# Whole-tensor loads, a pause in the load queue, and squares moved to the GpSimd engine, in a talking-heads attention and FFN kernel

## Chip, cores, metric

The kernel runs on one core of a Trainium2 chip; the sessions ran on different chips. The metric is device microseconds of that core for one execution. Executions of this kernel scatter more than those of many others: in six sessions the kernel before took between 602.3 and 613.0 us, without a run in the slower, disturbed state (runs in the undisturbed one are called "fast"). Ratios are computed as the mean time of one kernel's fast runs over the mean of the other's fast runs of the same rounds, with a 95% interval, so a ratio is not quite the ratio of the medians that are quoted beside it.

Engine names: PE is the matmul engine and PEld its weight loads, DVE the vector engine, ACT the scalar engine, POOL the GpSimd engine, SP the sync engine, which here only issues transfers.

## The reference

```python
# q, k, v: (8, 12, 448, 64) f32; w_pre, w_post: (12, 12)
def attention(q, k, v, w_pre, w_post):
    scores = (q @ k.transpose(0, 1, 3, 2)) / sqrt(64)
    scores = einsum('bhij,hg->bgij', scores, w_pre)        # mix the heads before the softmax
    attn = softmax(scores, axis=-1)
    attn = einsum('bhij,hg->bgij', attn, w_post)           # and again after it
    return attn @ v
# x: the attention output as (3584, 768); w_in: (768, 2048); w_out: (2048, 768)
def ffn(x, w_in, w_out):
    h = maximum(x @ w_in, 0.0)
    return (h * h) @ w_out
```

Inputs and output are f32; inside, the kernel works in bf16 with f32 accumulation.

## The kernel before

The 448 queries of a batch are 45 tiles of 10 queries; the program advances two tiles at a time. I call this a **double step** (ds), numbered from 0; a batch is 22.5 of them. For each tile:

- `score_pair` computes scores for a block of 128 queries and copies them to SBUF as `S` (half the copies on ACT, half on DVE).
- `gather` moves, for 10 queries, the scores of all 12 heads from `S` to 120 partitions of a buffer `G`: an SBUF-to-SBUF DMA of 105 KB in packets of 896 bytes. There are 12 `G` buffers, so gathers are issued 10 tiles ahead.
- `mix` multiplies `G` by the head-mixing weights (tile `m_ps`), ACT takes the exponential (`e_sb`) with its row sum, DVE the reciprocal (`rc`), POOL normalises (`d`). Two double steps later, `unmix` applies the second mixing (`at_ps`, copied by DVE to `at`).
- Attention times v (`ot_ps`, copied by ACT to `xt`), then the FFN: `h_ps`, relu (`hr`), square (`h`), `o_ps`. For the first batch the FFN's first half is done in pieces of 160, 160 and 128 queries as soon as these are ready.

q, k, v and the weights come from DRAM as f32 and become bf16 on the way: such casting transfers are issued by POOL, and they share one queue, called q0 below. Gathers are issued by SP (queue q1) or ACT (queue q10). q and k of a batch land in one staging buffer each (`qst`, `kst`), and PE transposes them (the **turn**, tile `tr_ps`). The turn of the second batch is due at double step 15, that of the third at 29 or 30.

PE and POOL take their work in the order of the program here (the traces below show it: a mix at 71.3 us stands behind transposes that wait until 69.8 us, and v is issued at 23.4 us, behind the first normalisation). So where in the program a load is issued decides when POOL gets to it.

```python
    def load(t, src, b, h0=0, h1=H):                 # heads h0..h1 of q, k or v
        nc.gpsimd.dma_start(out=t[0:PR, h0:h1, :, :].rearrange("p h r d -> p h (r d)"),
                            in_=src[b, h0:h1, :, :].rearrange("h (p r) d -> p h (r d)", r=R))
    ...
    def load_v(b, x):                                # thirds; load_qk the same, k and q in turn
        if x == 0:
            vs[b] = stage_tile("v", 2)
        load(vs[b], v, b, 4 * x, 4 * x + 4)
    def load_w1(x): ...                              # eighths of w_in, 384 KB each as bf16
    def load_w2(x): ...                              # eighths of w_out
    ...
        # in ffn1_unit, n = 160, 160, 128 queries for the first batch, S = 448 later
        square = nc.vector if n < S and ft % 4 else nc.gpsimd
        square.tensor_tensor(out=h2ts[(b, ft)][:, c0:c1], in0=hr[:, 0:n], in1=hr[:, 0:n], op=ALU.mult)
    ...
    def gather(k):
        ...
        eng = nc.scalar if b == 0 and k % 2 else nc.sync
        eng.dma_start(out=g[OFF:OFF + H * n, :], in_=Sb[(b, blk)][x:x + n, :, :])
    ...
        # at_load(i, f): f is issued before tile i; -1 is ahead of the first double step
        for x in range(2):
            at_load(-1, load_w1, x)
        for x in range(3):
            at_load(-1, load_v, 0, x)
            at_load(44 + x, load_v, 1, x)
        for x in range(2, 8):
            at_load(-1, load_w1, x)
        for x in range(8):
            at_load(18 + 2 * x + (6 if x > 3 else 0), load_w2, x)
        for x in range(6):
            at_load(6 + 2 * x, load_qk, 1, x)        # second batch
            at_load(46 + 2 * x, load_qk, 2, x)       # third batch
        ...                                          # later batches alike
        gathers_for(-1)                              # the first gathers
        for n in range(NPAIR, 2 * NPAIR):
            score_pair(n)                            # six more score pairs
        spin(8)                                      # matmuls whose result is not used
        for f in loads.get(-1, []):
            f()
        for ds in range(nd + LAG):
            for i in (2 * ds, 2 * ds + 1):
                for f in loads.get(i, []):
                    f()
            ...                                      # turn, unmix, attention times v as due
            scores_for(ds, ...)
            if now2:
                mix(ds)
            gathers_for(ds)
            ...
            fill(share)                              # FFN work
```

The softmax here doesn't subtract the row's maximum and nothing guards it: scores larger than these inputs give would overflow.

Of the kernel before, what the change touches and what calls it, by code (L numbers as in the profile page):

```python
# [14 lines left out]
B, H, S, D = 8, 12, 448, 64  # L15
DMODEL = H * D
DFF = 2048
NPAIR = H // 2
# [4 lines left out]
NT = 45  # L23
# [19 lines left out]
def kernel(  # L43
# [11 lines left out]
    nc = tc.nc  # L55
    P = nc.NUM_PARTITIONS
# [12 lines left out]
    def stage_tile(name, bufs):  # L69
        return stage.tile([P, H, R, D], BF16, name=name, tag=name, bufs=bufs)  # L70

    def load(t, src, b, h0=0, h1=H):
        nc.gpsimd.dma_start(out=t[0:PR, h0:h1, :, :].rearrange("p h r d -> p h (r d)"),
                            in_=src[b, h0:h1, :, :].rearrange("h (p r) d -> p h (r d)", r=R))

    staged, vs = {}, {}
# [58 lines left out]
    w1 = [wts.tile([P, NPAIR, DFF // 4], BF16, name=f"w1_{x}") for x in range(4)]  # L135
# [3 lines left out]
    def shared_half():  # L139
        return wts.tile([P, half2], BF16, name="w2_1", tag="w2_1", bufs=1)  # L140

    def w2_part(x):
        return w2[x][:, :].rearrange("p (c m) -> p c m", m=DMODEL)
# [63 lines left out]
    def av_units(b, part):  # L207
        return [(800, lambda cp=cp: av_unit(b, part, cp)) for cp in range(2)]

    def load_v(b, x):  # L210
        if x == 0:
            vs[b] = stage_tile("v", 2)
        load(vs[b], v, b, 4 * x, 4 * x + 4)

    def load_qk(b, x):
        if x == 0:
            kst = stage_tile("kst", 1)
            staged[b] = (stage_tile("qst", 1), kst)
        u, w = x // 2, 1 - x % 2
        load(staged[b][w], k if w else q, b, 4 * u, 4 * u + 4)  # L220

    def load_w1(x):
        n = DFF // 4
        h = NPAIR // 2
        c = x % 2 * h
        nc.gpsimd.dma_start(out=w1[x // 2][:, c:c + h, :],
                            in_=moe_w_in[128 * c:128 * c + 128 * h, n * (x // 2):n * (x // 2) + n].rearrange(
                                "(c p) f -> p c f", p=P))

    def load_w2(x):  # L230
        n = DFF // 8
        c = x % 4 * 2
        if x == 4:
            w2[1] = shared_half()
        nc.gpsimd.dma_start(out=w2_part(x // 4)[:, c:c + 2, :],
                            in_=moe_w_out[n * x:n * x + n, :].rearrange("(c p) m -> p c m", p=P))

    def ffn1_unit(b, ft, half, c0=0, c1=S):
        if half == 0:
            h_open[0] = bank("h_ps")  # L240
        ps = h_open[0]
        n = c1 - c0
        for c2 in range(3 * half, 3 * half + 3):
            nc.tensor.matmul(ps[:, 0:n], lhsT=w1[ft // 4][:, c2, ft % 4 * 128:ft % 4 * 128 + 128],  # L244
                             rhs=xts[b][:, c2, c0:c1], start=(c2 == 0), stop=(c2 == NPAIR - 1))
        if half == 0:
            return
        if (b, ft) not in h2ts:
            h2ts[(b, ft)] = ffnp.tile([P, S], BF16, name="h2", tag="h2", bufs=FT + 1)
        hr = ffnp.tile([P, S], F32, name="hr", tag="hr", bufs=2)  # L250
        if n < S and ft % 2:
            nc.vector.tensor_scalar_max(out=hr[:, 0:n], in0=ps[:, 0:n], scalar1=0.0)
        else:
            nc.scalar.activation(out=hr[:, 0:n], in_=ps[:, 0:n], func=ACT.Relu)  # L254
        square = nc.vector if n < S and ft % 4 else nc.gpsimd
        square.tensor_tensor(out=h2ts[(b, ft)][:, c0:c1], in0=hr[:, 0:n], in1=hr[:, 0:n], op=ALU.mult)  # L256

    h_open, o_open, osbs = {}, {}, {}
# [75 lines left out]
    def gather(k):  # L334

        b, t = steps[k]
        blk, tl = divmod(t, TPB)
        n = min(IQ, S - IQ * t)
        x = BLK_OFF[blk] + IQ * tl
        g = gts[k % len(gts)]  # L340
        eng = nc.scalar if b == 0 and k % 2 else nc.sync
        eng.dma_start(out=g[OFF:OFF + H * n, :], in_=Sb[(b, blk)][x:x + n, :, :])
        Gs[k] = g

# [61 lines left out]
    def spin(n):  # L406
        pss = [bank("spin_ps") for _ in range(2)]
        for _ in range(n):
            for z in (0, 64):
                rhs = ident[z:z + 64, 0:64].unsqueeze(1).to_broadcast([64, S // 64, 64])  # L410
                for x in (0, 64):
                    nc.tensor.matmul(pss[z // 64][x:x + 64, 0:S], lhsT=ident[z:z + 64, 0:64], rhs=rhs,
                                     start=True, stop=True)

    steps = [(b, t) for b in range(B) for t in range(NT)]
    with tc.manual_schedule(engines={PE, POOL}):
# [10 lines left out]
        def at_load(i, f, *args):  # L427
            loads.setdefault(i, []).append(lambda: f(*args))

        for x in range(2):  # L430
            at_load(-1, load_w1, x)
        for x in range(3):
            at_load(-1, load_v, 0, x)
            at_load(44 + x, load_v, 1, x)
        for x in range(2, 8):
            at_load(-1, load_w1, x)
        for x in range(8):
            at_load(18 + 2 * x + (6 if x > 3 else 0), load_w2, x)
        for x in range(6):
            at_load(6 + 2 * x, load_qk, 1, x)  # L440
            at_load(46 + 2 * x, load_qk, 2, x)
        for b in range(1, B):
            if b + 2 < B:
                for x in range(6):
                    at_load(NT * b + 22 + 2 * x, load_qk, b + 2, x)
            if b + 1 < B:
                for x in range(3):
                    at_load(NT * b + 34 + 2 * x, load_v, b + 1, x)
        nd = len(steps) // 2
        issued, gathered = [2 * NPAIR], [0]  # L450
        blocks = [(b, blk) for b in range(B) for blk in range(4)]
        starts = [NT * b + TPB * blk for b, blk in blocks] + [len(steps)]

        def scores_for(ds, most):
            tile = 2 * ds + AHEAD + 2
            blk = sum(tile >= x for x in starts) - 1
            if blk + 1 >= len(blocks):
                want = NPAIR * len(blocks)
            elif ds < 2 * NPAIR:
                want = 2 * NPAIR + 1 + ds  # L460
            elif blk in (3, 4):
                want = NPAIR * 4 + 2 * max(0, ds - FIRST_TURN[0])
            else:
                into, size = tile - starts[blk] - 2, starts[blk + 1] - starts[blk] - 2
                want = NPAIR * (blk + 1) + -(-NPAIR * into // size)
            want = min(want, issued[0] + most, NPAIR * min(blk + 2, len(blocks)))
            k = min(2 * ds + 8, len(steps) - 1)
            want = max(want, needs(steps[k]))
            while issued[0] < want and issued[0] % NPAIR < turned.get(issued[0] // (4 * NPAIR), 0):
                score_pair(issued[0])  # L470
                issued[0] += 1
# [6 lines left out]
                gathered[0] += 1  # L478

        gathers_for(-1)  # L480
        for n in range(NPAIR, 2 * NPAIR):
            score_pair(n)
        spin(8)
        for f in loads.get(-1, []):
            f()
        for ds in range(nd + LAG):
# [21 lines left out]
            if old2:  # L508
                unmix(ds - LAG)
                for b1, t1 in old2:  # L510
                    ends = PARTS[b1 % 2]
                    if t1 + 1 in ends:
# [3 lines left out]
                        if b1 == 0:  # L516
                            c = (IQ * ends[part], min(IQ * ends[part + 1], S))
# [47 lines left out]
```

## Time and profile before

| | us |
|---|---|
| median of the first 3 runs | 607.46 (605.88 to 608.25) |
| run in which the profile below was taken | 602.29 (span of the core 600.3) |
| a second profile of the same kernel, taken later | 609.92 (span 607.9) |

The head of the page of the kernel before: the span, then each engine's busy time, its share of the span and its instructions.

```profile
span 600.3 us, 27220 instructions
PE 557.1 (93%) x11346; PEld 316.7 (53%) x11346; DVE 432.8 (72%) x1123; ACT 395.5 (66%) x1196; POOL 397.0 (66%) x579
```

The chain of waits (the work that ended last, followed back from the end: start, duration, what) of the kernel before starts with the first loads and a few score copies, and then shows this:

```profile
17.82 6.77 DMA G<-S
24.61 0.80 ACTq L342
27.05 0.43 PE m_ps L351 x4
```

The chain stands for 6.77 us on one gather, while w_in and v move beside it; ACT issues one more gather (0.80 us); the first mix follows. The view of waits from 17 to 60 us says what ACT did meanwhile: it waited for that transfer in one piece.

```profile
engine line waited for: us in total, times, longest us
ACT S L325 <- DMA G<-S: 7.4, 1, 7.4
```

### The profile page before, as it was taken

To read this page: it belongs to the slowest core of one execution; us is meant where nothing else is said; L and a number is where in the kernel's file an instruction comes from. 1 tells how busy PE (TensorE), PEld (TensorE's weight loads), DVE (VectorE), ACT (ScalarE), POOL (GpSimd) and SP (SyncE) were. 2 spreads that over 40 slices of the span, in tenths; PEclk is the share of its full clock that TensorE was granted. 3 is DMA by queue.
4 is the path that set the end of the run, shared out by engine and by line. 5 is a ranking of instruction groups with operands and counts; after the bars stand their busy time and mean duration, and the time that the engine had idled before them with its cause. 6 is when DMAs were issued, how large, how long until landed. Compare 5 with 4: busy or idle time off the path is not lost.

```text
span 600.3 us, 27220 instructions
## 1 busy us (share of the span) xinstructions
PE 557.1 (93%) x11346; PEld 316.7 (53%) x11346; DVE 432.8 (72%) x1123; ACT 395.5 (66%) x1196; POOL 397.0 (66%) x579
## 2 busy tenths in 40 slices
PE   4698878988999999999999899999999999999996
PEld 3266555644655555545645455545655555555554
DVE  5488999987987688777786688777887787755101
ACT  2487677577778667876578656886678767962420
POOL 7288568466579945995479934996478846882440
PEclk9899999999999999999999999999999999999999
DMA  9999779589456965687446865588543655322002
GB/s 133 224 202 213 158 148 185 90 120 211 105 119 101 151 143 125 113 135 153 119 94 107 134 156 115 89 146 148 123 98 68 118 143 119 80 63 71 24 24 68
DMA packets 90912, 74.12 MB, mean 123 GB/s; under 512 B 6309, under 2 KB 87717, under 8 KB 90789
## 3 DMA queue, kind: packets, MB, share of 16 engines
q1 hardware_dynamic: 48982, 47.20, 33.2%
q0 software_dynamic: 38816, 22.81, 29.2%
q10 hardware_dynamic: 2990, 2.37, 1.2%
q8 instruction: 88, 1.44, 1.0%
q14 instruction: 36, 0.29, 0.1%
HBM read 45.63 MB, written 11.01 MB: 94 GB/s over the span
## 4 chain that ended last, share of the span: by engine, by line
PE 65%; POOL 10%; DVE 9%; DMA 7%; ACT 5%; issue 2%; ACTq 0%; DVEq 0%; POOLq 0%
PE o_ps L277 22%; PE h_ps L244 18%; PE at_ps L382 7%; PE ot_ps L193 6%; DMA G<-S 6%; PE m_ps L351 5%; POOL d L360 5%; DVE at L387 4%; PE s_ps L322 3%; POOL h L256 3%; PE tr_ps L170 3%; ACT e_sb L356 2%; ACT xt L204 2%; DVE S L325 2%; DMA qst<-in_q_dram 1%
## 5 line engine op out<-in xcount | busy, mean ns | idle before, releaser
L360 POOL TENSOR_SCALAR d<-e_sb,rc 128x448 bf16<-128x448 f32 x360 | 227.6, 644 | 158.5 <-DVE rc L358 156.6
L387 DVE CAST at<-at_ps 112x480 bf16<-112x480 f32 x360 | 219.2, 649 | 44.3 <-PE at_ps L382 42.0
L356 ACT ACTIVATE e_sb<-m_ps 128x448 f32<-128x448 f32 x360 | 195.8, 558 | 20.4 <-POOL d L360 9.9
L244 PE MATMUL h_ps<-xt,w 128*128 128x448 bf16 (+2 forms) x960 | 163.0, 316 | 3.6 <-DVE at L387 2.2
L277 PE MATMUL o_ps<-w,h 128*128 128x384 bf16 (+1 forms) x1024 | 161.6, 327 | 0.9 <-ACT xt L204 0.5
L325 ACT CAST S<-s_ps 128x448 bf16<-128x448 f32 x186 | 97.2, 540 | 74.0 <-PE s_ps L322 59.0
L244 PEld LDWEIGHTS <-w 128*128 128x128 bf16 x960 | 79.2, 98 | 80.2 <-issue 31.2
L277 PEld LDWEIGHTS <-h 128*128 128x128 bf16 (+1 forms) x1024 | 82.8, 101 | 72.0 <-issue 26.4
L256 POOL TENSOR_TENSOR h<-hr 128x448 bf16<-128x448 f32 (+2 forms) x124 | 109.1, 887 | 17.1 <-ACT hr L254 17.1
L325 DVE CAST S<-s_ps 128x448 bf16<-128x448 f32 x186 | 111.5, 613 | 3.3 <-PE s_ps L322 1.8
L382 PE MATMUL at_ps<-post,d 60*64 60x60 bf16 x5760 | 84.8, 194 | 7.3 <-POOL d L360 5.8
L382 PEld LDWEIGHTS <-d 60*64 60x64 bf16 x5760 | 63.6, 108 | 48.1 <-issue 18.7
L351 PE MATMUL m_ps<-G,pre 64*64 64x448 bf16 x720 | 77.5, 355 | 11.2 <-DVE at L387 2.6
L254 ACT ACTIVATE hr<-h_ps 128x448 f32<-128x448 f32 (+2 forms) x136 | 68.7, 511 | 27.5 <-PE h_ps L244 12.1
L356 ACT ACTIVATION_READ_ACCUMULATOR e_sb<-m_ps 128x1 f32 x360 | 78.1, 217 | 0.0
L204 ACT ACTIVATE xt<-ot_ps,bvec 128x160 bf16<-128x160 f32 (+3 forms) x144 | 44.6, 384 | 47.6 <-PE ot_ps L193 37.7
L322 PE MATMUL s_ps<-kT,qT 64*64 64x448 bf16 x768 | 70.4, 360 | 5.0 <-ACT S L325 3.9
L358 DVE RECIPROCAL rc<-sm 128x1 f32<-128x1 f32 x360 | 50.1, 154 | 33.1 <-ACT e_sb L356 31.2
L284 DVE COPY osb<-o_ps 128x384 f32<-128x384 f32 x48 | 26.0, 546 | 40.5 <-PE o_ps L277 40.4
L193 PE MATMUL ot_ps<-at,v 112*64 112x160 bf16 (+4 forms) x1152 | 46.1, 229 | 1.6 <-DVE at L387 1.4
L193 PEld LDWEIGHTS <-v 112*64 112x64 bf16 x1152 | 38.5, 109 | 14.6 <-issue 14.1
L351 PEld LDWEIGHTS <-pre 64*64 64x64 bf16 x720 | 28.2, 106 | 29.1 <-issue 27.2
(43 smaller groups left out, 239.2 us busy)
## 6 DMA issues: line engine op xcount, KB each, us to landing
G<-S SPq DMA_DIRECT2D x324, 105.0 KB
kst<-in_k_dram POOLq DMA_DIRECT2D x24, 224.0 KB, 6.1
qst<-in_q_dram POOLq DMA_DIRECT2D x24, 224.0 KB, 5.9
v<-in_v_dram POOLq DMA_DIRECT2D x24, 224.0 KB, 5.8
w<-in_moe_w_in_dram POOLq DMA_DIRECT2D x8, 384.0 KB, 16.6
w<-in_moe_w_out_dram POOLq DMA_DIRECT2D x8, 384.0 KB, 15.1
out_dram<-osb SPq DMA_DIRECT2D x8, 336.0 KB
out_dram<-osb SPq DMA_DIRECT2D x8, 288.0 KB
```

Source lines behind the costliest of these rows:

```text
L193: nc.tensor.matmul(ps[64 * hh:64 * hh + 64, TW * y + c0:TW * y + 2 + n], lhsT=vs[b][0:PR, g, r, :], rhs=at[0:PR, r, g, c0:2 + n], start=(y ...
L244: nc.tensor.matmul(ps[:, 0:n], lhsT=w1[ft // 4][:, c2, ft % 4 * 128:ft % 4 * 128 + 128], rhs=xts[b][:, c2, c0:c1], start=(c2 == 0), stop=( ...
L254: nc.scalar.activation(out=hr[:, 0:n], in_=ps[:, 0:n], func=ACT.Relu)
L256: square.tensor_tensor(out=h2ts[(b, ft)][:, c0:c1], in0=hr[:, 0:n], in1=hr[:, 0:n], op=ALU.mult)
L277: nc.tensor.matmul(dst, lhsT=h2ts[(b, ft)][:, mt * 128:mt * 128 + ROWS[mt]], rhs=w2_part(ft // 8)[:, ft % 8, n2 * 384:(n2 + 1) * 384], sta ...
L322: nc.tensor.matmul(pss[hh][z:z + 64, 0:S], lhsT=qTs[b][rs, p, q0:q0 + 64], rhs=kTs[b][rs, p, :], start=True, stop=True)
L325: copy(out=Sb[(b, blk)][:, 2 * p + hh, :], in_=pss[hh][:, 0:S])
L351: nc.tensor.matmul(pss[y][64 * x:64 * x + 64, 0:S], lhsT=pre[rows, :], rhs=gs[x][rows, :], start=True, stop=True)
L356: nc.scalar.activation(out=e[:, :], in_=pss[y][:, 0:S], func=ACT.Exp, scale=SCALE, accum_out=sm[:, 0:1])
L360: nc.gpsimd.tensor_scalar(out=d[:, 0:S], in0=e[:, :], scalar1=rc[:, 0:1], scalar2=-1.0 / S, op0=ALU.mult, op1=ALU.add)
L382: nc.tensor.matmul(us[x][z:z + 64, c:c + HR], lhsT=d[rows, PR * r + z:PR * r + z + 64], rhs=post[rows, :], start=True, stop=True)
L387: nc.vector.tensor_copy(out=dst, in_=src)
```

## The change

Its intent is fourfold. One transfer per tensor (and per quarter of the weights) instead of pieces saves POOL issue time. A pause in the loads, from the first quarter of w_in until the first normalisation, gives the first gathers the DMA engines for themselves. Gathers of the first batch move from ACT to SP (all but two), and fewer score pairs precede the first double step, so ACT is free earlier. Of the first batch's 48 squares, 36 instead of 12 go to POOL, because DVE is full there.

The diff, cut to its core:

```diff
-    def load_v(b, x):
-        if x == 0:
-            vs[b] = stage_tile("v", 2)
-        load(vs[b], v, b, 4 * x, 4 * x + 4)
+    def load_v(b):
+        vs[b] = stage_tile("v", 2)
+        load(vs[b], v, b)
 ... (load_qk: whole q or k; load_w1 and load_w2: quarters instead of eighths)
-        square = nc.vector if n < S and ft % 4 else nc.gpsimd
+        square = nc.vector if n < S and ft % 4 == 1 else nc.gpsimd
 ...
-        eng = nc.scalar if b == 0 and k % 2 else nc.sync
+        eng = nc.scalar if k in (1, 3) else nc.sync
 ...
+        at_load(-1, load_w1, 0)
+        at_load(2, load_v, 0)                          # the pause: ds 1, not -1
+        for x in range(3):
+            at_load(4 + 2 * x, load_w1, x + 1)         # the pause: ds 2 to 4, not -1
         for x in range(2):
-            at_load(-1, load_w1, x)
-        for x in range(3):
-            at_load(-1, load_v, 0, x)
-            at_load(44 + x, load_v, 1, x)
-        for x in range(2, 8):
-            at_load(-1, load_w1, x)
-        for x in range(8):
-            at_load(18 + 2 * x + (6 if x > 3 else 0), load_w2, x)
-        for x in range(6):
-            at_load(6 + 2 * x, load_qk, 1, x)
-            at_load(46 + 2 * x, load_qk, 2, x)
+            at_load(12 + 4 * x, load_qk, 1, 1 - x)     # k at 12, q at 16
+            at_load(46 + 6 * x, load_qk, 2, 1 - x)
+        for x in range(4):
+            at_load((20, 24, 32, 36)[x], load_w2, x)
+        at_load(44, load_v, 1)
 ... (later batches alike)
-        issued, gathered = [2 * NPAIR], [0]
+        issued, gathered = [NPAIR + 3], [0]
 ...
-                want = 2 * NPAIR + 1 + ds
+                want = min(NPAIR + 5 + 2 * ds, 2 * NPAIR + ds)
 ...
-        for n in range(NPAIR, 2 * NPAIR):
+        for n in range(NPAIR, issued[0]):
             score_pair(n)
-        spin(8)
+        spin(4)
```

More of the change, by code (lines that the diff above doesn't have):

```diff
@@ L208, in av_units, with load_qk @@
         return [(800, lambda cp=cp: av_unit(b, part, cp)) for cp in range(2)]
-    def load_v(b, x):
-        if x == 0:
-            vs[b] = stage_tile("v", 2)
-        load(vs[b], v, b, 4 * x, 4 * x + 4)
-    def load_qk(b, x):
-        if x == 0:
-            kst = stage_tile("kst", 1)
-            staged[b] = (stage_tile("qst", 1), kst)
-        u, w = x // 2, 1 - x % 2
-        load(staged[b][w], k if w else q, b, 4 * u, 4 * u + 4)
+    def load_v(b):
+        vs[b] = stage_tile("v", 2)
+        load(vs[b], v, b)
+    def load_qk(b, w):
+        if w:
+            staged[b] = (stage_tile("qst", 1), stage_tile("kst", 1))
+        load(staged[b][w], k if w else q, b)
     def load_w1(x):
         n = DFF // 4
-        h = NPAIR // 2
-        c = x % 2 * h
-        nc.gpsimd.dma_start(out=w1[x // 2][:, c:c + h, :],
-                            in_=moe_w_in[128 * c:128 * c + 128 * h, n * (x // 2):n * (x // 2) + n].rearrange(
-                                "(c p) f -> p c f", p=P))
+        nc.gpsimd.dma_start(out=w1[x][:, :, :], in_=moe_w_in[:, n * x:n * x + n].rearrange("(c p) f -> p c f", p=P))
     def load_w2(x):
-        n = DFF // 8
-        c = x % 4 * 2
-        if x == 4:
+        n = DFF // 4
+        c = x % 2 * 4
+        if x == 2:
             w2[1] = shared_half()
-        nc.gpsimd.dma_start(out=w2_part(x // 4)[:, c:c + 2, :],
+        nc.gpsimd.dma_start(out=w2_part(x // 2)[:, c:c + 4, :],
                             in_=moe_w_out[n * x:n * x + n, :].rearrange("(c p) m -> p c m", p=P))
@@ L428, in at_load @@
             loads.setdefault(i, []).append(lambda: f(*args))
+        at_load(-1, load_w1, 0)
+        at_load(2, load_v, 0)
+        for x in range(3):
+            at_load(4 + 2 * x, load_w1, x + 1)
         for x in range(2):
-            at_load(-1, load_w1, x)
-        for x in range(3):
-            at_load(-1, load_v, 0, x)
-            at_load(44 + x, load_v, 1, x)
-        for x in range(2, 8):
-            at_load(-1, load_w1, x)
-        for x in range(8):
-            at_load(18 + 2 * x + (6 if x > 3 else 0), load_w2, x)
-        for x in range(6):
-            at_load(6 + 2 * x, load_qk, 1, x)
-            at_load(46 + 2 * x, load_qk, 2, x)
+            at_load(12 + 4 * x, load_qk, 1, 1 - x)
[3 more added lines that the diff above has]
+        at_load(44, load_v, 1)
         for b in range(1, B):
             if b + 2 < B:
-                for x in range(6):
-                    at_load(NT * b + 22 + 2 * x, load_qk, b + 2, x)
+                for x in range(2):
+                    at_load(NT * b + 22 + 6 * x, load_qk, b + 2, 1 - x)
             if b + 1 < B:
-                for x in range(3):
-                    at_load(NT * b + 34 + 2 * x, load_v, b + 1, x)
+                at_load(NT * b + 36, load_v, b + 1)
         nd = len(steps) // 2
-        issued, gathered = [2 * NPAIR], [0]
+        issued, gathered = [NPAIR + 3], [0]
         blocks = [(b, blk) for b in range(B) for blk in range(4)]
```

## The prediction

> **What bounds the kernel now.** The page gives a span of 600.3 us, PE 93% busy, DVE 72%, ACT and POOL 66%. By stretches (busy time of each engine), PE is 97 to 99% busy from 160 to 560 us: bound by PE. Idle PE lies before 160 us: 12.8 of the first 25 us busy, then 56 of 67 us between 53 and 120 us. Three limits:
> 1. 0 to 29 us: the chain of waits runs from the loads of q and k over the S copies to a gather of 6.8 us (17.8 to 24.6): ACT issues five gathers, then sits idle 7.4 us until one lands. The first mix starts at 26.5 us, the first normalisation on POOL at 29.0. w1 and v, 3.7 MB as written, are queued beside the gathers.
> 2. 29 to 50 us: a double step takes 2.04 us. ACT is full: copy 0.53, two exponentials with read-outs, and 0.80 us to issue a gather. DVE needs 1.8 to 1.9.
> 3. 53 to 120 us: DVE is over 90% busy (56.7 of 60 us from 60 on); its 36 squares of the first batch take 0.41 to 0.44 us each (14.9 us in all).
>
> **What changes.**
> - Startup: only the first quarter of w1 is in flight before the gathers, ACT issues two gathers, not five, and three score pairs instead of six precede the first double step. I estimate the gather at 3 us and the first mix at 21 us: 5.3 us gained, critical.
> - Double steps of the first batch: no 0.80 us issue on ACT; DVE becomes the limit at about 1.9 us. Twelve steps gain about 0.7 us net of larger POOL issues.
> - Issue time on POOL: 0.73 us now per third; I estimate 1.0 to 1.1 us for a whole tensor (144 elements take 0.53). About 25 us of POOL time vanish, nearly all off the critical path.
> - Squares: 24 move to POOL. DVE loses about 10 us between 53 and 118 us; POOL gains 12 us (0.45 to 0.59 each) and loses about 6 us of issue. POOL nears 90% in places: I count 4 of PE's 11 idle us. The Trainium skill (GPSIMD Engine Reference, "Engine selection") makes POOL about 2 times slower for two-input operations; the trace shows 0.45 against 0.30 us uncontended.
> - Cost: the DMA engines are saturated until 60 us, and the pause idles them some 3 us. v, three quarters of w1, then k and q of the second batch share one queue; at its 131 GB/s (7.48 MB in 57 us) q would land at about 56 us (estimate), while the second batch's turn wants it at 53: minus 1.5 us.
> - After 160 us: nothing.
>
> **Prediction:** 607.5 - 5.3 - 0.7 - 4 + 1.5 = 599; I put the middle at **598 us**, range 590 to 605. Faster by over 2%: 0.30; within 2%: 0.67; slower: 0.03.
>
> **What the profile would show if right:** first mix at 20 to 22 us, no ACT idle of several us on a gather; steps of 1.9 us up to the first attention-value product; DVE below 85% between 60 and 110 us with POOL above 80%.
>
> **What would make it wrong.** Gathers on one queue falling behind a saturated load queue (idle ACT or PE on G in 25 to 60 us) would eat the startup gain, as would PE waiting on the second batch's k or q. POOL in fixed order could hold the squares' buffers and stall ACT's relu and PE: then squares gain nothing. If DVE's relief reaches PE in full, the gain is over 12 us.

## More of the kernel before

A second profile of the same kernel, taken later: 609.92 us (span 607.9). The two profiles of one kernel differ by 7.6 us, most of it before 160 us. The first, which I had when I predicted, happened to be a quick run. For comparisons step by step I use the second, the **repeat**; it lies inside the range of this kernel's fast runs.

An average over the span hides the stages. The view by windows gives, for each stretch, its length, each engine's busy time (with instructions), the granted PE clock, the DMA share and the GB/s moved.

```profile
core 0: us, PE busy (x) PEld busy (x) DVE busy (x) ACT busy (x) POOL busy (x), PEclk, DMA share, GB/s
15.00:24.00 9.00, 6.33 (x72) 2.54 (x69) 5.40 (x10) 3.05 (x6) 2.79 (x4) 1.00 1.31 210
24.00:45.00 21.00, 18.00 (x458) 11.11 (x457) 14.55 (x41) 16.20 (x49) 13.52 (x22) 0.92 1.06 215
62.00:85.00 23.00, 18.82 (x446) 12.64 (x441) 21.71 (x57) 15.75 (x50) 12.51 (x20) 1.00 0.79 150
160.00:560.00 400.00, 390.94 (x8021) 214.10 (x8018) 298.10 (x747) 285.09 (x868) 279.03 (x401) 1.00 0.59 116
```

From 160 us on PE is 98% busy (390.94 of 400), so its work sets the pace there. Before that the limits are others. From 15 to 45 us the DMA share is over 1: this share adds up the time that packets took, divided by 16 engines, so above 1 it says that more packets than engines were in flight on average (1.31 is about 21 packets). From 62 to 85 us DVE is busy 21.71 of 23 us.

The DMA view lists the packets, megabytes and packet time of each queue. From 15 to 24 us:

```profile
## 3 DMA queue, kind: packets, MB, share of 16 engines
q0 software_dynamic: 2388, 1.66, 122.7%
q1 hardware_dynamic: 105, 0.09, 3.9%
q10 hardware_dynamic: 125, 0.11, 3.7%
```

The loads (q0) moved 1.66 MB in these 9 us, the gathers 0.20 MB. And from 24 to 45 us, the queues, and then the loads of k and q of the second batch (pieces, size, us from issue to landing):

```profile
q0 software_dynamic: 2717, 2.12, 66.7%
q1 hardware_dynamic: 1406, 1.16, 21.3%
q10 hardware_dynamic: 1420, 1.17, 16.8%
kst<-in_k_dram POOLq DMA_DIRECT2D x3, 224.0 KB, 13.0
qst<-in_q_dram POOLq DMA_DIRECT2D x3, 224.0 KB, 13.8
```

No wait of PE for k or q of the second batch shows in this kernel, in either profile: they are there when the turn is due.

## The result, and the profile after

| | median of fast runs, us | range | n |
|---|---|---|---|
| before, same rounds | 607.86 | 605.88 to 609.34 | 4 |
| after | 616.21 | 614.89 to 617.03 | 4 |

The ratio is 1.0138 (1.0101 to 1.0174): the changed kernel is 1.4% slower. The prediction of 598 us, with a range up to 605, was wrong in sign.

The head of the page after, and the same windows:

```profile
span 615.1 us, 27146 instructions
PE 560.9 (91%) x11330; PEld 322.0 (52%) x11330; DVE 426.0 (69%) x1099; ACT 393.5 (64%) x1196; POOL 372.9 (61%) x551
```

```profile
15.00:24.00 9.00, 6.37 (x73) 4.60 (x72) 4.97 (x12) 5.27 (x15) 1.79 (x3) 0.81 0.42 95
24.00:45.00 21.00, 16.26 (x447) 10.18 (x440) 14.70 (x41) 13.09 (x41) 14.08 (x22) 0.92 1.15 198
62.00:85.00 23.00, 15.10 (x360) 11.95 (x360) 12.61 (x30) 8.83 (x29) 8.26 (x15) 0.78 0.73 143
160.00:560.00 400.00, 393.37 (x8191) 213.56 (x8191) 306.16 (x774) 293.60 (x900) 270.34 (x385) 1.00 0.60 118
```

After 160 us the two kernels are alike (PE 98% busy in both). From 62 to 85 us PE lost a fifth of its busy time and DVE, ACT and POOL lost a third to nearly a half, so all of them waited for something; the granted PE clock fell with it, to 0.78. From 15 to 24 us the DMA share is 0.42 instead of 1.31. The queues of those 9 us:

```profile
q1 hardware_dynamic: 741, 0.62, 32.7%
q10 hardware_dynamic: 260, 0.22, 8.1%
q0 software_dynamic: 15, 0.01, 0.9%
```

The gathers moved 0.84 MB instead of 0.20, which was the aim. But the load queue moved 0.01 MB instead of 1.66; by its packet records it was empty from 15.6 to 25.3 us, 9.7 us in all, while in the kernel before it never stood empty for 0.5 us between 8 and 70 us. From 24 to 45 us, with all gathers on q1:

```profile
q0 software_dynamic: 3611, 2.77, 88.8%
q1 hardware_dynamic: 1603, 1.33, 25.5%
kst<-in_k_dram POOLq DMA_DIRECT2D x1, 672.0 KB, 25.7
qst<-in_q_dram POOLq DMA_DIRECT2D x1, 672.0 KB, 27.4
```

The gathers got 1.33 MB through instead of 2.33, and the whole k and q took 25.7 and 27.4 us from issue to landing. The chain of waits after, first its start and then the stretch to the turn:

```profile
16.19 4.27 DMA G<-S
20.51 0.78 PE m_ps L344 x4
...
29.87 8.64 DMA G<-S
...
42.41 27.36 DMA qst<-in_q_dram
69.82 0.96 PE tr_ps L170 x16
71.34 0.47 PE m_ps L344 x3
```

The first mix now starts at 20.5 us. Later the chain stands for 8.64 us on a gather, and then for 27.36 us, from 42.4 to 69.8, on one transfer: q of the second batch. The last two lines show who needed it: PE's transposes for the turn, and behind them in program order the mix of double step 15. PE's own waits from 14 to 165 us, the longest two:

```profile
PE tr_ps L170 <- DMA qst<-in_q_dram: 9.4, 2, 6.7
PE m_ps L344 <- DMA G<-S: 8.1, 8, 1.7
```

To see what each stage gained or lost, I take the start of the first exponential of a double step from ACT's timeline, in the repeat of the kernel before and in the profile after, in us:

| double step | before (repeat) | after | after minus before |
|---|---|---|---|
| 0 | 27.58 | 21.27 | -6.3 |
| 4 | 35.63 | 29.47 | -6.2 |
| 9 | 46.83 | 46.67 | -0.2 |
| 14 | 60.48 | 60.10 | -0.4 |
| 15 | 63.44 | 71.78 | +8.3 |
| 16 | 67.37 | 76.59 | +9.2 |
| 28 | 106.58 | 113.82 | +7.2 |
| 44 | 158.27 | 167.19 | +8.9 |
| 179 (last) | 552.21 | 559.44 | +7.2 |

This is the account by stages, from one run of each kernel. The gain at the start is real, and holds for four double steps; by double step 9 it is gone; at double step 15, the turn, 8.7 us are lost in one place; the squares' stage (16 to 28) gives 2.0 back, the next turn takes about as much, and the rest changes little. The last line equals the difference of the two spans (615.1 - 607.9 = 7.2). How far such rows can be trusted shows when the first profile of the kernel before takes the place of the repeat: the turn (14 to 15) takes 2.95 us in the one and 2.96 in the other, but steps 0 to 12 take 25.1 and 28.8 us.

### The profile page after: what moved, and what is told of

It is laid out like the page before. It is cut to its first block, busy times and chain, and to the rows that moved or that the text cites. A ratio compares the mean times of both kernels' runs of the same rounds, so it can differ in the third digit from the quotient of the medians.

```text
span 615.1 us, 27146 instructions
## 1 busy us (share of the span) xinstructions
PE 560.9 (91%) x11330; PEld 322.0 (52%) x11330; DVE 426.0 (69%) x1099; ACT 393.5 (64%) x1196; POOL 372.9 (61%) x551
## 4 chain that ended last, share of the span: by engine, by line
PE 69%; DMA 16%; DVE 6%; ACT 4%; POOL 2%; issue 2%; ACTq 0%; SPq 0%; DVEq 0%; POOLq 0%
PE o_ps L270 22%; PE h_ps L237 20%; DMA G<-S 9%; PE at_ps L375 8%; DMA qst<-in_q_dram 7%; PE ot_ps L193 6%; PE m_ps L344 5%; PE tr_ps L170 4%; PE s_ps L315 4%; DVE at L380 3%; POOL d L353 2%; ACT e_sb L349 1%; DVE S L318 1%; ACT xt L204 1%; ACT S L318 1%
## 5 line engine op out<-in xcount | busy, mean ns | idle before, releaser
L349 ACT ACTIVATE e_sb<-m_ps 128x448 f32<-128x448 f32 x360 | 195.0, 557 | 31.2 <-PE m_ps L344 28.0
L249 POOL TENSOR_TENSOR h<-hr 128x448 bf16<-128x448 f32 (+2 forms) x148 | 118.3, 810 | 17.2 <-ACT hr L247 17.2
L237 PEld LDWEIGHTS <-w 128*128 128x128 bf16 x960 | 80.5, 99 | 77.9 <-issue 29.2
L344 PE MATMUL m_ps<-G,pre 64*64 64x448 bf16 x720 | 80.3, 360 | 18.1 <-DMA G<-S 8.1
L315 PE MATMUL s_ps<-kT,qT 64*64 64x448 bf16 x768 | 69.8, 364 | 1.9 <-ACT S L318 0.9
L277 DVE COPY osb<-o_ps 128x384 f32<-128x384 f32 x48 | 26.0, 547 | 40.7 <-PE o_ps L270 40.6
L344 PEld LDWEIGHTS <-pre 64*64 64x64 bf16 x720 | 28.8, 107 | 37.3 <-issue 31.6
## 6 DMA issues: line engine op xcount, KB each, us to landing
qst<-in_q_dram POOLq DMA_DIRECT2D x7, 672.0 KB, 12.3
```

What stands on the lines that cost most here:

```text
L237: nc.tensor.matmul(ps[:, 0:n], lhsT=w1[ft // 4][:, c2, ft % 4 * 128:ft % 4 * 128 + 128], rhs=xts[b][:, c2, c0:c1], start=(c2 == 0), stop=( ...
L315: nc.tensor.matmul(pss[hh][z:z + 64, 0:S], lhsT=qTs[b][rs, p, q0:q0 + 64], rhs=kTs[b][rs, p, :], start=True, stop=True)
L344: nc.tensor.matmul(pss[y][64 * x:64 * x + 64, 0:S], lhsT=pre[rows, :], rhs=gs[x][rows, :], start=True, stop=True)
L349: nc.scalar.activation(out=e[:, :], in_=pss[y][:, 0:S], func=ACT.Exp, scale=SCALE, accum_out=sm[:, 0:1])
```

## The experiments

My first theory, after reading the traces, was: **the pause leaves the load queue empty for over 8 us in a stage in which it has no slack, and the loads behind it are late at the turn.** Rivals were: the whole-tensor transfers (a third used to be visible early; a whole lands late), the single gather queue, and the squares on POOL, which runs in program order. All kernels gave the reference's result.

### First group: undo one part of the change

No pause: v and the rest of w_in are issued at once.

```diff
-        at_load(2, load_v, 0)
+        at_load(-1, load_v, 0)
         for x in range(3):
-            at_load(4 + 2 * x, load_w1, x + 1)
+            at_load(-1, load_w1, x + 1)
```

> The changed kernel, with v and all four quarters of w1 issued before the first double step again (still whole transfers). Theory P (the pause is the cause: it leaves the load queue empty from about 15 to 24 us, so that q of the second batch lands at 69.8 us, after its turn is due): q of the second batch lands before 60 us, the PE wait of 6.7 us on it is gone, the first mix comes at 23 to 25 us instead of 20.5, total 599 to 605 us. Rival W (whole transfers are the cause) and rival Q (gathers on one issuing queue): still 611 us or more.

Measured: 610.8 us, ratio to before 1.0066 (1.0006 to 1.0127). The jump at the turn is gone: double step 15 follows 14 by 2.4 us instead of 11.7. It isn't fully back at the time of before: the steps up to 9 are slow, and PE still waits 2.7 us for q of the third batch. Its load queue, too, runs empty for 5.7 us, only later (38.3 to 44.0 us), as k is not issued before 42.3 us. About half of the loss goes with the pause while one gather queue remains (each ratio is to the kernel before in its own rounds). The forecast of 599 to 605 us was missed; the total lies nearer to the 611 us of the rivals.

Pieces again, issued back to back at the places of the changed kernel.

```diff
-        load(vs[b], v, b)
+        for h in (0, 4, 8):
+            load(vs[b], v, b, h, h + 4)
 ... (the same for q and k; w_in and w_out in halves)
```

> The changed kernel, each tensor in thirds and each weight quarter in halves again, issued back to back at the same places, so with the pause. Rival W: the first third of q lands early enough for the first turn, 4 to 6 us of the 8.8 us stall at double step 15 go, and the 2.7 us at step 29 go as well: 607 to 610 us. Theory P: the queue is in order and still late, so at most 3 us better: 613 us or more.

Measured: 618.21 us, 1.0173 (1.0106 to 1.0241). Transfer size is not the cause of the lost time, but it decides where the time is lost: double step 15 now follows 14 by 3.5 us instead of 11.7, PE has no wait for q or k at all, and 8.2 us pass between 18 and 19 instead (2.1 in both the repeat and the changed kernel), behind a gather of 15.3 us.

Two gather queues again.

```diff
-        eng = nc.scalar if k in (1, 3) else nc.sync
+        eng = nc.scalar if b == 0 and k % 2 else nc.sync
```

> The changed kernel with the first batch's odd gathers issued by ACT again. Theory Q (a gather on SP's queue alone gets a smaller share of the DMA engines beside a full load queue): the loss of 7.3 us between double steps 4 and 9 goes, gathers move about 105 GB/s there instead of 63; but the loads then get less, so the stall on q at step 15 grows by as much and the total stays within 3 us of 616. If gathers do not care which engine issues them: steps 4 to 9 stay slow, and the 0.8 us issue on ACT makes them slower still.

Measured: 620.05 us, 1.0196 (1.0129 to 1.0264). It did not help. Its first exponential starts at 23.6 us, so the pause ends later as well, and the stall at the turn is there again, on k first and then on q (PE's waits from 50 to 80 us):

```profile
PE tr_ps L170 <- DMA kst<-in_k_dram: 6.4, 1, 6.4
PE tr_ps L170 <- DMA qst<-in_q_dram: 3.0, 1, 3.0
```

Squares back on DVE.

```diff
-        square = nc.vector if n < S and ft % 4 == 1 else nc.gpsimd
+        square = nc.vector if n < S and ft % 4 else nc.gpsimd
```

> The changed kernel with 36 of the first batch's 48 squares on DVE again, as before the change. If the squares on POOL gain what the step times suggest (the lag behind the old kernel shrinks from 11.7 to 8.9 us between double steps 16 and 22): 2 to 4 us slower than the changed kernel, 618 to 620 us. If they cost time: faster, below 615 us.

Measured: 614.75 us (median of its three fast runs; one was slow), 1.0120 (1.0054 to 1.0187), not distinguishable from the changed kernel. Inside the stage the busy time moves as it was meant to. Double steps 16 to 28 take 39.1 us here and 37.2 us in the changed kernel (39.2 before), but this gain of 2 us is no larger than what single profiles scatter: with the squares on POOL they take 38.9 us in the kernel with two queues above and 40.7 us in the kernel with POOL squares alone below. The windows from 76 to 106 us, first this kernel, then the changed one:

```profile
76.00:106.00 30.00, 24.06 (x616) 17.02 (x617) 28.84 (x74) 21.33 (x70) 16.93 (x26) 1.00 0.86 157
```

```profile
76.00:106.00 30.00, 25.29 (x633) 18.44 (x630) 24.80 (x68) 22.47 (x75) 20.43 (x36) 1.00 0.82 146
```

DVE falls from 28.84 to 24.80 us busy of 30, POOL rises from 16.93 to 20.43, and PE does 1.2 us more work.

### Second group: one part alone in the kernel before

The pause alone (pieces, six score pairs and two gather queues stay):

```diff
-            at_load(-1, load_v, 0, x)
+            at_load(2, load_v, 0, x)
 ...
-            at_load(-1, load_w1, x)
+            at_load(2 + x // 2 * 2, load_w1, x)
```

> The old kernel with the pause alone: v at double step 1, the last three quarters of w1 at steps 2 to 4, pieces as in the old kernel, gathers on two queues. Theory P: the load queue is empty for some 8 us before the first normalisation, the first mix comes 2 to 3 us earlier, and what was gained is given back by the late q and k of the second batch at step 15: 608 to 614 us. If the pause is harmless: 603 to 606 us.

Measured: 615.63 us, 1.0123 (1.0078 to 1.0168). This one edit costs as much as the whole change. It gains nothing at the start here (27.5 us against 27.6 in the repeat), since ACT and PE still do the old amount of work ahead of it, and it loses steadily to double step 12 (60.9 against 56.4). I had taken it for the same mechanism throughout; it isn't quite. The load queue is nearly empty from 15 to 24 us (0.17 MB on q0), as in the changed kernel, and stays empty until 31.2 us (13.7 us in all, against 9.7), since the first normalisation comes later. And POOL, in program order, now also issues the nine late pieces, and those of k and q, between normalisations, and stands still for landings: the three thirds of v take 2.2 us to issue, and five waits for w_in to land take 0.7 to 1.5 us each.

Whole transfers alone (load functions and places of the changed kernel, but v and all of w_in at -1):

```diff
-        for x in range(3):
-            at_load(-1, load_v, 0, x)
+        at_load(-1, load_v, 0)
-        for x in range(2, 8):
-            at_load(-1, load_w1, x)
+        for x in range(3):
+            at_load(-1, load_w1, x + 1)
 ... (load_v, load_qk, load_w1, load_w2 and all later places as in the change)
```

> The old kernel with whole transfers alone, at the changed kernel's places but without the pause. Theory W: single transfers of 672 KB hold up the gathers and make the second and third batches' turns wait for whole tensors: 610 us or more. If whole transfers only save issue time on POOL: 606 to 608 us, unchanged.

Measured: 607.9 us, 1.0000 (0.9954 to 1.0046). Neither loss nor gain.

One gather queue alone, in the kernel before:

```diff
-        eng = nc.scalar if b == 0 and k % 2 else nc.sync
+        eng = nc.scalar if k in (1, 3) else nc.sync
```

> The old kernel with the first batch's gathers, but for the second and fourth, issued by SP. Theory Q: beside the full load queue the gathers get about 63 GB/s instead of 105, the mixes of the first ten double steps wait for them by 5 us or more, while ACT is freed early (first mix 2 us earlier): 608 to 614 us. If the queue does not matter, ACT's freed 0.8 us per step and the earlier first mix give 602 to 605 us.

Measured: 610.43 us, 1.0025 (0.9980 to 1.0070). PE waits 7.4 us for gathers between 24 and 62 us, where the repeat of the kernel before waits for 0.2 us, yet double step 36 starts at 132.8 us, against 133.6 in the repeat. Its first exponential comes 2.4 us earlier (25.1), double step 9 is 1.4 us behind (48.2 against 46.8), and 12 is 1.2 us ahead again (55.2 against 56.4): the waits use up the early start, and no lasting loss shows. The loads get more of the DMA engines meanwhile (1.39 MB on q0 from 24 to 35 us instead of 1.24).

POOL squares alone, in the kernel before:

```diff
-        square = nc.vector if n < S and ft % 4 else nc.gpsimd
+        square = nc.vector if n < S and ft % 4 == 1 else nc.gpsimd
```

> The old kernel with 36 instead of 12 of the first batch's squares on POOL. By the step times of the changed kernel: 2 to 4 us gained between double steps 15 and 22, 604 to 606 us. By the comparison with the squares put back on DVE, which showed no difference: 607 to 609 us.

Measured: 610.23 us, 1.0023 (0.9975 to 1.0071). No gain that can be told from zero, although the load moved as the prediction wanted: from 60 to 110 us DVE is busy for 40.2 of 50 us (47.3 in the repeat) and POOL for 38.3 (34.2), but PE for 40.4 (41.6). So a full DVE is not shown to be what held PE there.

### Third group: does the order of the loads settle it?

If only k and q are late, they can go first: w_in quarter 1 at tile 4, k at 6, q at 8, the last two quarters of w_in at 12 and 16.

```diff
-        for x in range(3):
-            at_load(4 + 2 * x, load_w1, x + 1)
+        at_load(4, load_w1, 1)
         for x in range(2):
-            at_load(12 + 4 * x, load_qk, 1, 1 - x)
+            at_load(6 + 2 * x, load_qk, 1, 1 - x)
+            at_load(12 + 4 * x, load_w1, 2 + x)
```

> The changed kernel with the same pause and the same transfers, but k and q of the second batch queued ahead of the last two quarters of w1. Theory P: the queue's 9 empty microseconds are paid by whatever stands last when it is due. q now lands by 56 us, the waits of 8.2 us on k and q at the second batch's turn (step 15) go; up to 4 us return as a wait of the first FFN matmuls on the last quarter of w1: 608 to 612 us. Rival (the turn's stall is only where other delays surface): still 614 us or more.

Measured: 620.08 us, 1.0171 (1.0126 to 1.0216). The stall at the turn is indeed gone: double step 15 starts at 62.0 us and 18 at 75.2, both ahead of the repeat (63.4 and 77.1). Then 10.9 us pass between the starts of 18 and 19. The chain of waits and the waits from 60 to 90 us:

```profile
68.45 16.41 DMA G<-S
```

```profile
ACT S L318 <- DMA G<-S: 8.6, 1, 8.6
PE h_ps L237 <- ACT S L318: 7.8, 1, 7.8
```

ACT may not overwrite `S` until a gather has read it; that gather took 16.41 us, and PE stood behind ACT. **The stall moved, to another transfer.**

The same with two gather queues:

```diff
-        eng = nc.scalar if k in (1, 3) else nc.sync
+        eng = nc.scalar if b == 0 and k % 2 else nc.sync
```

> The same with the first batch's odd gathers on ACT's queue again. Theory Q with P: the gathers keep up in steps 4 to 9 (4 to 6 us gained there), the loads are later by as much, so that the wait on q or w1 grows: within 3 us of the kernel with k and q first. If the loads still land in time: 603 to 606 us.

Measured: 613.04 us, 1.0071 (1.0023 to 1.0118), the best kernel with a pause, and still slower than before. The stall between 18 and 19 is gone (2.1 us), so it took the single gather queue as well as the new order; 7.9 us pass between 23 and 24 instead (3.8 in the repeat). With k and q first, two gather queues are worth 1%, in intervals that do not overlap; in the order of the changed kernel they gained nothing.

The same as the first of this group, with v at -1:

```diff
-        at_load(2, load_v, 0)
+        at_load(-1, load_v, 0)
```

> k and q first, and v issued before the first double step, so that the load queue is empty for about 4 us instead of 9. Theory P: each microsecond of queue time won comes back at step 15 or at w1: 3 to 4 us faster than with k and q first alone, less about 1 us for a later first mix: 605 to 609 us.

Measured: 618.0 us, 1.0140 (1.0101 to 1.0179). Between double steps 18 and 19, 12.8 us pass, behind a gather of 16.1 us, though v no longer waits behind the pause. The load queue was not empty for 4 us, as expected, but for 9.1 (20.2 to 29.2 us; 9.4 in the first of this group): the next load, a quarter of w_in, still waits for double step 2, so the earlier v moved the gap more than it closed it. The last packet of q does come 4 us earlier (52.7 us against 56.8), but q was not what the stall waited for.

The kernel before once more, without an edit, for one profile:

> The old kernel once more, for its profile: the profiled run of before took 602.3 us where the median is 608. If the difference between the two profiles is partly luck of that run, this one shows a gather wait of 3 to 5 us between double steps 36 and 44 (about 150 us), as most of the other profiles do and that one does not, and a span of 604 to 607 us.

Measured: 609.92 us. This is the repeat used above. It showed that 7.6 us of what I had first put down to the change, of a difference of spans of 14.8 us, was the difference of two runs of the same kernel. (The record names the chip of the second alone, so a difference of chips is not excluded.)

### Fourth group: the other corner, and later weights

No pause and two gather queues: the changed kernel with whole transfers, fewer score pairs and POOL squares, but v and w_in issued ahead of the first double step and both gather queues, as before.

```diff
-        at_load(2, load_v, 0)
+        at_load(-1, load_v, 0)
         for x in range(3):
-            at_load(4 + 2 * x, load_w1, x + 1)
+            at_load(-1, load_w1, x + 1)
 ...
-        eng = nc.scalar if k in (1, 3) else nc.sync
+        eng = nc.scalar if b == 0 and k % 2 else nc.sync
```

> The changed kernel without the pause and with the first batch's odd gathers on ACT's queue: of the change, whole transfers, squares on POOL and fewer first score pairs are left. Theory P with Q: no long wait on q, k or gathers before step 20; within 0.5% of the old kernel, 605 to 611 us. If a third cause in the changed kernel costs time: 613 us or more.

Measured: 607.74 us, 1.0005 (0.9960 to 1.0049). With this the four corners are complete, everything else being as in the changed kernel:

| ratio to before | one gather queue | two gather queues |
|---|---|---|
| with the pause | 1.0138 (the change) | 1.0196 |
| without | 1.0066 | 1.0005 |

With two queues the pause costs 1.9%, and these intervals are far apart. With one queue it costs 0.7%, and those overlap a little. (The profiled runs of the two kernels with two queues were the slowest of theirs, 622.87 and 612.80 us, so the table rests on the times, and their profiles serve for the mechanism alone.) How the queues share the engines shows from 24 to 35 us, both without the pause; first two queues, then one:

```profile
q0 software_dynamic: 1244, 1.25, 67.1%
q1 hardware_dynamic: 706, 0.59, 20.6%
q10 hardware_dynamic: 642, 0.53, 14.4%
```

```profile
q0 software_dynamic: 1409, 1.41, 76.1%
q1 hardware_dynamic: 861, 0.72, 25.2%
q10 hardware_dynamic: 105, 0.09, 2.3%
```

With two queues the gathers got 1.12 MB through, with one 0.81 MB, and the loads correspondingly 1.25 and 1.41 MB. The Trainium skill ("DMA: Bandwidth & Descriptors", section "Queues, rings and completion order") says that each DMA engine takes turns between the queue rows that have work, packet by packet. The amounts agree: two rows against the loads' one would get more turns than one row against one. (The traces do not record which engine moved a packet, so the turns themselves do not show.)

k and q first, and w_out later (tiles 32, 36, 40, 42):

```diff
-            at_load((20, 24, 32, 36)[x], load_w2, x)
+            at_load((32, 36, 40, 42)[x], load_w2, x)
```

> k and q first, and w2 issued at tiles 32, 36, 40 and 42 instead of 20, 24, 32 and 36. Debt theory: 1.6 MB less stand in the queue before step 16, the stall of 8.8 us at step 19 shrinks to under 2 us, and 6 to 9 us of the 10 us excess go: 610 to 614 us. If the stall at step 19 has another cause: still 617 us or more.

Measured: 619.01 us, 1.0173 (1.0127 to 1.0219). The stall between 18 and 19 is gone too: double steps 15, 19 and 23 start 1.9, 1.0 and 1.4 us ahead of the repeat. Then 12.3 us pass between 23 and 24, where the late w_out meets the next batch's v and k (waits from 80 to 105 us):

```profile
ACT S L318 <- DMA G<-S: 8.7, 1, 8.7
PE ot_ps L193 <- ACT S L318: 8.0, 1, 8.0
```

The same, with the first batch's odd gathers on ACT again, but for four of them:

```diff
-        eng = nc.scalar if k in (1, 3) else nc.sync
+        eng = nc.scalar if b == 0 and k % 2 and (k < 4 or k > 11) else nc.sync
```

> The same, and the first batch's odd gathers from the thirteenth on go to ACT's queue. Theory Q: the gathers keep up from step 5 on, the loss of 6 us between steps 4 and 9 shrinks to 2 to 3 us: 604 to 609 us, the first candidate that could beat both. If the queue does not matter: as with late w2 alone or slower by ACT's issue time.

Measured: 619.37 us (median of its four fast runs), 1.0164 (1.0115 to 1.0213).

No pause, with the late w_out and the same gather line (edits to the changed kernel):

```diff
-        at_load(2, load_v, 0)
+        at_load(-1, load_v, 0)
         for x in range(3):
-            at_load(4 + 2 * x, load_w1, x + 1)
+            at_load(-1, load_w1, x + 1)
 ...
-            at_load((20, 24, 32, 36)[x], load_w2, x)
+            at_load((32, 36, 40, 42)[x], load_w2, x)
 ...
-        eng = nc.scalar if k in (1, 3) else nc.sync
+        eng = nc.scalar if b == 0 and k % 2 and (k < 4 or k > 11) else nc.sync
```

> No pause, w2 late, odd gathers from the thirteenth on ACT's queue, the order of loads as in the old kernel. The first exponential at 25 us, gathers four to eleven slow on one queue beside the load queue (2 to 4 us lost by step 5), no stall after that: 604 to 609 us.

Measured: 620.58 us, 1.0194 (1.0161 to 1.0228). Delaying w_out costs the same stall even without the pause (10.7 us between 23 and 24). In this it is like the pause: a load was held back, and a later step waited.

### Fifth group: a version that beats both?

The corner without pause and with two queues starts its first exponential at 26.8 us; ACT issues a fifth gather just before. Taking that one off ACT, in that kernel and in the kernel before:

```diff
-        eng = nc.scalar if b == 0 and k % 2 else nc.sync
+        eng = nc.scalar if b == 0 and k % 2 and k != 9 else nc.sync
```

> The changed kernel without the pause and on two queues, but the tenth gather on SP's queue, so that ACT issues four gathers before its next copies instead of five. If the fifth waits for a landing and blocks ACT: the first exponential comes 2 to 3 us earlier than with five (24 to 25 us), and with both queues kept at work 1 to 2 us of it are left at step 10: 604 to 608 us. If not: unchanged from the kernel with five.

> The old kernel with the tenth gather on SP's queue, nothing else. If the fifth gather blocks ACT: first exponential at 25 to 26 us instead of 28, 0.2 to 0.4% faster in all, 605 to 608 us, which five rounds may just fail to tell from the old kernel. If the gathers are then short of share: no gain left by step 5.

Measured: 613.43 us (median of its five fast runs, which scatter from 606.7 to 615.8; a sixth was slow), 1.0030 (0.9976 to 1.0083), and 610.91 us, 1.0018 (0.9981 to 1.0055). The first exponential does come earlier (24.7 instead of 26.8 us, and 26.9 instead of 27.6), and the gain is given back: in the first of the two, double step 2 starts at 32.3 us, as in the corner without this edit (32.4). No kernel that I ran beats the kernel before.

## Why the prediction was wrong

**The step that failed most is "Cost": that q of the second batch "would land at about 56 us", at a price of "minus 1.5 us".** q landed at 69.8 us, and the turn cost 8.7 us. The mechanism was named and is the right one; its size was not. Two more terms of the sum failed: the double steps (0.7 us gained forecast, 5.6 lost measured), whose risk was named but given no cost, and the squares (4 us gained forecast, no gain shown). Against the repeat of the kernel before, term by term, in us:

| term | predicted | measured (profiles) |
|---|---|---|
| startup | -5.3 | -6.3 |
| twelve double steps (0 to 12) | -0.7 | +5.6 |
| turn of the second batch (14 to 15) | +1.5 | +8.7 |
| squares (16 to 28) | -4 | -2.0 |
| all other steps, the third batch's turn included | 0 | +1.2 |
| sum | -8.5 | +7.2 |

*Startup: right.* The gather took 4.27 us (3 predicted, 6.77 before), and the first mix began at 20.5 us (21 predicted).

*Double steps: right for the first few, then wrong.* From 1 to 4 a step took 1.83 us (1.9 predicted, 2.0 before). From 4 to 9 it took 3.44 us. The prediction put the shorter POOL issues and ACT's freedom into the sum, and gathers "falling behind a saturated load queue" only into the list of what could go wrong, at a cost of zero in the sum. They did fall behind: of PE's 8.1 us of waits for `G`, 5.2 lie between 29 and 48 us. It is not the single queue alone: with two queues and the pause, the stretch from 4 to 9 loses 2.2 us to the repeat instead of 6.0, and ACT instead of PE waits for a gather, 3.6 us in one piece.

*The cost of the pause: the mis-sized term.* Of the DMA engines, the 3 us of idling came true: from 15 to 17.7 us hardly a packet moved. But after that only gathers moved, and the load queue stayed empty for 9.7 us, as v is issued only behind the first normalisation, at 23.4 us. By 24 us the load queue had moved 2.16 MB, against 3.64 in the repeat, and the last packet of q moved at 69.4 us, against 56.0 there. The turn waited 1.5 us for k and 6.7 us for q. PE runs in program order, so the mix behind the turn waited too, and with it every other engine: hence the window from 62 to 85 us.

Where the estimate of 56 us went wrong can be worked out (estimates from the numbers given). v, three quarters of w_in, k and q are 4.42 MB. From v's first packet, at 25.3 us, they take until 59 us at the 131 GB/s that I assumed, so the start was about 3 us later than I had allowed for. By 69.4 us the queue had moved not 4.42 but 5.36 MB: 0.93 MB of w_out, which is issued behind q and which I did not count, are 7 us at that rate. The remaining 3 us are the rate, 121 GB/s instead of 131. This is arithmetic: no run has the changed order of loads with w_out alone held back.

Part of q's lateness is not in the average rate. Packet sizes tell the tensors apart (512 bytes are q, k and v, 1,536 are w_out): from 45 to 62 us 383 packets of w_out, issued behind q, had already moved, while the last 57 packets of q went between 66 and 70 us. So the queue is not worked off strictly in order, and it would fit that some DMA engines were well ahead of others. Which engine moved a packet is not recorded. The gathers post 10 completion packets each, which suggests that they run on 10 of the 16 engines, and that these 10 lag; that is an inference that no run here tests, and other causes are not excluded.

*Was it the order or the amount?* In these kernels the order and the size of the loads decided who waited, not whether somebody waited: pieces, or k and q first, remove the stall at the turn, and 8.2 and 10.9 us pass four double steps later; with w_out later this stall goes too, and 12.3 us pass five double steps on. Two gather queues also remove the stall of k and q first, and the total falls by 1%, but a part of it comes back at double step 23. What these kernels share is that the load queue, which has work queued without a break in the kernel before, stood empty for 9 to 14 us near the start, or was filled later than it could have been. That this missing work is a debt, which the next consumer without slack pays, is my reading of these stalls. It is not shown: the one edit that lowered the missing amount by itself (v ahead of the first double step, 0.69 MB more moved by 24 us) gained 0.3%, within the intervals, and no kernel with an evenly paced schedule was tried.

*Squares: the load moved, the gain is not shown.* From 76 to 106 us DVE went to 83% (24.80 of 30 us), below the 85% predicted. POOL reached 68%, not the 80% predicted. The stage took 2.0 us less than in the repeat, not 4, and this is within what single profiles scatter; alone in the kernel before, the same edit took DVE to 80% and POOL to 77% and gained nothing. So the step "I count 4 of PE's 11 idle us" failed. The prediction cited the Trainium skill ("GPSIMD Engine Reference", "Engine selection") for POOL being about two times slower in such operations. The squares of 160 queries took 0.45 us on POOL, and 0.41 us on a crowded DVE, 0.30 on one that was not: a factor of 1.5 at most here.

*Issue times on POOL: right.* A whole tensor takes 0.97 to 0.99 us to issue (1.0 to 1.1 estimated), a third 0.73. The saving lay off the critical path, as said: whole transfers alone give a ratio of 1.0000.

*After 160 us nothing: right* (+7.2 at the last double step, +8.9 at double step 44).

What stays open: which DMA engines lag, why the double steps from 4 to 9 still lose time with two gather queues, and whether a load schedule without idle time and without crowding beats the kernel before.

## What to carry to other kernels

Before you hold a load back to favour something urgent, read how many bytes its queue moves in the time you take away, and who needs the last of them: here the queue had work without a break, and what was held back was missing at a later place that had no slack. Count also what is queued behind the load that you need: here some of it moved first. Moving the stalled load to the front only showed the next stall. And when one kernel's runs scatter by 1%, take a second profile of it before explaining a difference step by step: here half of the difference between the first two profiles was scatter.

## What the Trainium skill lacked or had wrong

- "DMA: Bandwidth & Descriptors", "Issuing engines are not separate DMA queues", says that starting transfers from several engines saves only the sequencers' time to issue them. Here it also changed how the DMA engines were shared: beside the same loads, gathers issued from two engines moved 1.12 MB in 11 us, from one 0.81 MB, while the loads moved 1.25 and 1.41 MB. This agrees with the page's own section on arbitration, and that sentence should name this effect as well.
- The same page, section "Bandwidth", advises batching transfers to at least 1 MiB. Going from 224 KB to 672 KB (and from 384 to 768 KB) per transfer, still short of that, changed nothing here that can be measured: ratio 1.0000 (0.9954 to 1.0046), and 1.22 MB on the load queue from 24 to 35 us against 1.24. These loads convert f32 to bf16 and ran beside gathers; no run tests them alone.
- The same page, section "Why a DMA increments its semaphore by 16 and not by 1", gives the rule for the number of engines, the largest up to 16 that divides the row counts of both sides; a gather goes from 10 rows to 120, which makes 10, and its 10 completion packets agree. I found no page that measures how large transfers of all 16 engines fare beside such ones: 383 packets of a later transfer had moved by 62 us, while 57 packets of an earlier one in the same queue moved only after 66 us.
- I found no page that warns that one kernel's profile may be far from its median: two profiles of the same kernel had spans of 600.3 and 607.9 us, both undisturbed as far as can be told (possibly on two chips).
